# Layer 2 of a two-layer mixture of experts written out by hand, and partial token tiles collected

## The chip, the cores and the metric

The kernel runs on one core of one Trainium2 chip. The metric is the device time of one execution in microseconds (us). Before the change the median of three runs is 539.6 us (539.29 to 540.68). The engines are TensorE (PE; its weight loads are listed as PEld), VectorE (DVE), ScalarE (ACT), GpSimd (POOL) and SyncE (SP), which here only issues DMAs.

## The reference, cut to what matters

An attention without softmax (the scores are multiplied by a decay) gives 2304 tokens of 512 numbers. They pass two layers of a mixture of eight experts: the first has a capacity, the second a skip gate. In both each token goes to the one expert with the highest logit.

```python
logits = x @ w_gate
expert_idx = np.argmax(logits, axis=1)
...
h = np.maximum(np.einsum('ecd,edf->ecf', disp, w1), 0.0)
y = np.einsum('ecf,efd->ecd', h, w2)
...
out[i] = gate_w[i] * y[expert_idx[i], pos[i]]
...
# second layer, on tokens with x @ w_skip > 0; the others keep x
h = np.maximum(xc[mask] @ w1[e], 0.0)
y[mask] = gate_w[mask, None] * (h @ w2[e])
...
out[do_compute] = xc + y
```

Each expert has `w1` of 512 x 1024 and `w2` of 1024 x 512; all numbers are float32.

## The kernel before, in words

Up to some 110 us the kernel computes the attention and the routing of layer 1; layer 1 runs to about 350 us, layer 2 to about 532. Tokens are scattered by an indirect DMA from GpSimd into one list per expert in DRAM (`xs1`, `xs2`), and gathered from there (`load_rows`, L691: `xb`, for the matmuls; `load_own`, L717: `rows`, with gate, token number and, in layer 2, the row itself).

*Positions.* The experts are taken in nine positions (`CAPS`, L31), each with a fixed number of rows: 160, 176, 316, 296, 292, 288, 276, 264, 256 in layer 1 and 176, 32, 324, 240, 172, 172, 156, 156, 144 in layer 2. Positions 0 and 1 are the same expert: 0 takes the rows that are known early, 1 the late ones; position 1 of layer 2 has 32 rows and a path of its own (`SMALL`, `small1`, `small2`). From position 2 on the experts come in order of their number of tokens, which `order` (L542) works out once a layer's routing is complete; `expert` (L681) has SyncE read an expert's number. `ends` writes a block of zero rows behind each list (`pad`, L488, an indirect DMA).

*Steps.* A position has eight steps f, one for each 128 of the 1024 hidden numbers. `s1` (L803) is the first matmul, `h` in PSUM, from which ScalarE makes the ReLU `hh` and, where it is wanted, VectorE the rest `hl`. `s2` (L867) is the second, accumulated in four PSUM tiles `y` (features by tokens), or, for 240 rows, in tiles of tokens (`token_major`). The weights come in units of 512 KB + 512 KB, each for two steps (`load_unit`, L736), five in flight.

*Precision.* Over 192 rows (`F32_MAX`) each float32 factor is split in a high and a low half of type fp32r, and three products are summed: `convert_unit` (L750) makes `hi` (ScalarE, L768) and `lo` (VectorE, L769) of both weights, `transposes` (L783) transposes the rows on VectorE and splits them likewise. Up to 192 rows plain float32 is used. For the positions in `PAIR` (L46: position 1 of layer 1, positions 4 to 7 of layer 2) the second matmul alone is split: both halves of `hh` lie side by side, so that `hi` takes 2C columns at once (L892) and `lo` C more (L893).

*The end of a position.* `evac` (L907) copies `y` to `yt`; `out` (L921) transposes `yt` by tiles of 128 tokens back to rows (`yr`), a tile being four transposes; the last tile of a position is partial. In layer 1 `post1` (L999) computes the scores for the next router (`logits4`, tile `M`; one transpose `Mt` for each token tile), scales the rows by the gate into `x2s` and `x2r` on ScalarE, and scatters both, one indirect DMA for each and each tile. In layer 2 `post2` (L1038) makes the row numbers `of` and `oi` on VectorE (L1050, L1051), then four multiply-adds for each tile (L1056) and one scatter to the output.

*Order.* One loop, `run` (L936), writes out both layers: loads, conversions, gathers, `s1` a step ahead, `s2`. Of this order GpSimd and SyncE keep what is written; TensorE, VectorE and ScalarE are ordered by the planner of the language, by its own costs. Each engine then works off its queue strictly in that order.

## Time and profile before

| | us |
|---|---|
| median of three runs | 539.6 |
| the profiled execution | 540.63 |
| its span, first to last instruction | 538.8 |
| TensorE busy | 514.2 |
| VectorE busy | 328.5 |
| ScalarE busy | 242.2 |
| GpSimd busy | 150.9 |

The mean granted TensorE clock was 0.989 of full speed. A matmul's listed time is longer than the distance to the next one, since they are pipelined: what a step costs is read from the starts of two like instructions, or from the chain of waits, which counts each up to the next.

### The profile page before, as it was taken

What the parts mean: (1) busy time and instruction counts of PE and PEld (TensorE: products, weight loads), DVE (VectorE), ACT (ScalarE), POOL (GpSimd) and SP (SyncE); (2) the same over time, 40 slices, a digit from 0 to 9 for tenths busy, and PEclk for the clock granted to TensorE, in tenths of its full rate; (3) what the DMA queues carried; (4) which work ended last, traced back from release to release, by engine and by line L of the source; (5) the groups of instructions that cost most, each with busy time, mean ns of one, the idle gap of its engine ahead of it and who ended that gap; (6) DMA issues with size and microseconds to landing.
All of it is one profiled execution on the core that took longest, in us unless ns stands there. A gap on an engine that the chain in (4) does not pass through costs nothing.

```text
span 538.8 us, 12402 instructions
## 1 busy us (share of the span) xinstructions
PE 514.2 (95%) x4439; PEld 480.9 (89%) x4439; DVE 328.5 (61%) x992; ACT 242.2 (45%) x448; POOL 150.9 (28%) x216
## 2 busy tenths in 40 slices
PE   7899999999999999999999999998989799999993
PEld 6779888798999999999999999997978689999993
DVE  5756769555775856667585957345667355565422
ACT  2344455243564655656474756234344324344220
POOL 3443747331403060323324242230302110110111
PEclk9999999999999999999999999999989899999998
DMA  8799996855994757584839474317899658788700
GB/s 195 159 204 200 237 233 165 301 192 179 298 285 134 233 167 201 170 230 134 246 112 273 138 245 129 119 46 209 259 350 321 195 197 262 250 276 283 259 25 28
DMA packets 133420, 109.65 MB, mean 203 GB/s; under 512 B 57398, under 2 KB 111030, under 8 KB 133350
## 3 DMA queue, kind: packets, MB, share of 16 engines
q1 hardware_dynamic: 127077, 94.70, 61.5%
q0 software_dynamic: 6272, 14.07, 7.1%
q8 instruction: 37, 0.61, 0.5%
q14 instruction: 34, 0.27, 0.2%
HBM read 93.44 MB, written 20.17 MB: 211 GB/s over the span
## 4 chain that ended last, share of the span: by engine, by line
PE 63%; issue 16%; DMA 8%; SPq 5%; POOL 3%; DVE 2%; ACT 2%; POOLq 0%; DVEq 0%; ACTq 0%
PE h L834 6%; PE h L833 6%; PE h L832 6%; PE y L899 6%; PE y L900 6%; PE y L898 6%; PE h L822 6%; PE yr L929 2%; DMA rows<-xs 2%; PE S L206 2%; PE O L248 2%; PE y L892 2%; PE y L895 2%; DMA r<-w1b 2%; POOL out L986 1%
## 5 line engine op out<-in xcount | busy, mean ns | idle before, releaser
L769 DVE TENSOR_TENSOR lo<-r,hi 128x1024 fp32r<-128x1024 f32 x92 | 112.2, 1223 | 58.3 <-ACT hi L768 57.7
L768 ACT CAST hi<-r 128x1024 fp32r<-128x1024 f32 x92 | 96.3, 1048 | 56.8 <-PE y L899 16.9
L899 PE MATMUL y<-hl,hi 128*128 128x316 f32 (+7 forms) x256 | 76.4, 299 | 0.0
L900 PE MATMUL y<-hh,lo 128*128 128x316 f32 (+7 forms) x256 | 76.2, 298 | 0.0
L898 PE MATMUL y<-hh,hi 128*128 128x316 f32 (+7 forms) x256 | 75.1, 298 | 0.0
L476 POOL DMA_INDIRECT xs<-x2s,idx x24 | 28.0, 1165 | 156.1 <-ACT hi L768 57.7
L837 ACT ACTIVATE hh<-h 128x316 fp32r<-128x316 f32 (+8 forms) x72 | 29.1, 404 | 63.9 <-PE h L834 63.6
L986 POOL DMA_INDIRECT out<-o,oi x17 | 19.7, 1157 | 131.4 <-DVE o L1056 128.4
L892 PE MATMUL y<-hh,hi 128*128 128x312 f32 (+2 forms) x160 | 49.4, 369 | 0.4
L899 PEld LDWEIGHTS y<-hl,hi 128*128 128x128 f32 x256 | 48.2, 188 | 0.3 <-DVE oi L1051 0.2
L900 PEld LDWEIGHTS y<-hh,lo 128*128 128x128 f32 x256 | 48.2, 188 | 0.3 <-issue 0.3
L838 DVE SCALAR_TENSOR_TENSOR hl<-h,hh 128x316 fp32r<-128x316 f32 (+8 forms) x72 | 31.9, 446 | 26.9 <-ACT hh L837 26.8
L898 PEld LDWEIGHTS y<-hh,hi 128*128 128x128 f32 x256 | 47.9, 188 | 0.0
L893 PE MATMUL y<-hh,lo 128*128 128x156 f32 (+2 forms) x160 | 38.5, 240 | 0.0
L209 DVE TENSOR_TENSOR P<-S,tab 128x512 f32<-128x512 f32 (+1 forms) x40 | 23.6, 632 | 15.4 <-PE S L206 15.1
L825 ACT ACTIVATE hh<-h 128x172 fp32r<-128x172 f32 (+2 forms) x40 | 12.4, 310 | 43.3 <-PE h L822 42.5
L892 PEld LDWEIGHTS y<-hh,hi 128*128 128x128 f32 x160 | 30.1, 188 | 1.4 <-DVE hh L826 1.1
L893 PEld LDWEIGHTS y<-hh,lo 128*128 128x128 f32 x160 | 30.5, 191 | 0.1
L895 PE MATMUL y<-hh,r 128*128 128x160 f32 (+2 forms) x192 | 29.9, 300 | 0.0
L986 POOL DMA_INDIRECT out<-x2r,si x24 | 27.7, 1153 | 7.3 <-issue 5.5
L895 PEld LDWEIGHTS y<-hh,r 128*128 128x128 f32 x192 | 27.2, 190 | 0.1
L929 PE MATMUL yr<-ident,yt 128*128 128x128 f32 (+11 forms) x156 | 24.4, 282 | 0.8 <-DVE o L1056 0.8
(613 smaller groups left out, 1268.8 us busy)
## 6 DMA issues: line engine op xcount, KB each, us to landing
r<-w1a SPq DMA_DIRECT2D x32, 512.0 KB
r<-w2a SPq DMA_DIRECT2D x32, 512.0 KB
r<-w1b SPq DMA_DIRECT2D x32, 512.0 KB
r<-w2b SPq DMA_DIRECT2D x32, 512.0 KB
k<-k SPq DMA_DIRECT2D x32, 128.0 KB
q<-q SPq DMA_DIRECT2D x16, 256.0 KB
v<-v SPq DMA_DIRECT2D x32, 128.0 KB
xb<-xs SPq DMA_DIRECT2D x12, 160.0 KB
```

Of the source, the lines that this page charges most:

```text
L768: nc.scalar.copy(hi, raw)
L769: nc.vector.tensor_sub(lo, raw, hi.bitcast(F32))
L822: nc.tensor.matmul(ps, w.r1[:, c, fc], s.xh[:, c, 0:C], start=(c == 0), stop=(c == 3))
L832: nc.tensor.matmul(ps, w.hi1[:, c, fc], s.xh[:, c, 0:C], start=(c == 0), stop=False)
L892: nc.tensor.matmul(s.y[d][:, 0:2 * C], w.hi2[:, f % 2, dc], s.hh[f].rearrange("p a c -> p (a c)"), start=a, stop=False)
L893: nc.tensor.matmul(y, w.lo2[:, f % 2, dc], s.hh[f][:, 0], start=False, stop=o)
L895: nc.tensor.matmul(y, w.r2[:, f % 2, dc], s.hh[f], start=a, stop=o)
L898: nc.tensor.matmul(y, wh, s.hh[f], start=a, stop=False)
L899: nc.tensor.matmul(y, wh, s.hl[f], start=False, stop=False)
L900: nc.tensor.matmul(y, wl, s.hh[f], start=False, stop=o)
L929: g.nc.tensor.transpose(ps[0:n, 128 * d:128 * d + 128], s.yt[:, d, 128 * k:128 * k + n], g.ident)
L986: r = g.nc.gpsimd.indirect_dma_start(out=g.oa["out"][:, :].rearrange("n (b d) -> (n b) d", b=parts), out_offset=IndirectOffsetOnAxis(ap=id ...
```

## The change

Four things are changed.

- Partial token tiles are collected. In groups of positions (`ENDS`: 0 and 1, 2 and 3, 4 to 6 of layer 1; 0 and 2, 4 to 6, 7 and 8 of layer 2) `evac` copies the rows beyond a multiple of 128 into a common tile `cy` (ScalarE); the last position of the group puts it out as one tile, and `load_own` gathers its rows from each expert of the group. In layer 1 the scores of `cy` take a `logits4` call of their own.
- The halves side by side stay in positions 4 and 5 of layer 2 (172 rows). The other three positions of `PAIR` use plain float32.
- Layer 2 has a routine of its own, `run2`, with conversions by halves (`convert_half`: 1 for `w1`, 2 for `w2`). In its context ScalarE and VectorE too keep the order that is written. TensorE is still ordered by the planner, and in layer 1 so are ScalarE and VectorE.
- `of` and the row numbers are computed by GpSimd, and `post(2)` of layer 2 is put out in two parts. `hold` copies the small position's result out of PSUM.

```diff
-TILES = {l: [(c + 127) // 128 for c in cs] for l, cs in CAPS.items()}
+ENDS = {1: [(0, 1), (2, 3), (4, 5, 6)], 2: [(0, 2), (4, 5, 6), (7, 8)]}
+TAIL = {l: {m[-1]: [(p, sum(CAPS[l][q] % 128 for q in m[:i])) for i, p in enumerate(m)] for m in ms} for l, ms in ENDS.items()}
+AT = {l: {p: o for m in ms.values() for p, o in m} for l, ms in TAIL.items()}
...
+def tail(lay, pos):
+
+    return sum(CAPS[lay][p] % 128 for p, _ in TAIL[lay].get(pos, []))
+
+
+TILES = {l: [c // 128 + (p in TAIL[l]) if p in AT[l] else (c + 127) // 128 for p, c in enumerate(cs)] for l, cs in CAPS.items()}
...
-PAIR = {1: (1,), 2: (4, 5, 6, 7)}
+PAIR = (4, 5)
...
+    k = C // 128
+    if T > k:
         nc.gpsimd.memset(s.rows[:, T - 1, GATE - c0:], 0.0)
...
+    if T > k:
+        for p, o in TAIL[lay].get(pos, [(pos, 0)]):
+            m = CAPS[lay][p]
+            n, a = m % 128, start_slot(lay, p) + m - m % 128
+            nc.sync.dma_start(out=s.rows[o:o + n, k], in_=xs[ds(expert(g, lay, p), 1), a:a + n, c0:c1].rearrange("o p w -> (o p) w"))
...
+def convert_half(g, u, i):
...
     if u >= 2 * UNITS:
         return
     lay, pos = user(u)
-    both = CAPS[lay][pos] > F32_MAX
-    if not both and max(pos, 1) not in PAIR[lay]:
+    if CAPS[lay][pos] <= F32_MAX and (i == 1 or lay == 1 or pos not in PAIR):
...
+    raw, shape = (t.r1, [128, 4, 256]) if i == 1 else (t.r2, [128, 2, 512])
+    if hasattr(t, f"hi{i}"):
         return
...
+    hi = g.wc.tile(shape, F32R, tag=f"hi{i}", name=f"hi{i}_{u}")
+    lo = g.wc.tile(shape, F32R, tag=f"lo{i}", name=f"lo{i}_{u}")
+    setattr(t, f"hi{i}", hi)
+    setattr(t, f"lo{i}", lo)
+    nc.scalar.copy(hi, raw)
+    nc.vector.tensor_sub(lo, raw, hi.bitcast(F32))
+
+
+def convert_unit(g, u):
+    convert_half(g, u, 1)
+    convert_half(g, u, 2)
...
-    def transposes(self, pos, cs=range(4)):
+    def transposes(self, pos, cs=range(4), apart=False):
...
-        if not f32:
+        if f32:
+            return
+
+        def high():
             nc.scalar.copy(s.xh[:, c], x)
+
+        def low():
             nc.vector.tensor_sub(s.xl[:, c], x, s.xh[:, c].bitcast(F32))
+
+        if apart:
+            return high, low
+        high()
+        low()
...
+    def pair(self, pos):
+        return self.lay == 2 and pos in PAIR
...
+        if pos in AT[self.lay]:
+            o, n = AT[self.lay][pos], C % 128
+            if o == 0:
+                self.cy = g.yp.tile([128, 4, 128], F32, tag="cy", name=f"cy{self.lay}_{pos}")
+            g.nc.scalar.copy(self.cy[:, :, o:o + n], s.yt[:, :, C - n:C])
+
+    def count(self, pos, k):
+
+        C = CAPS[self.lay][pos]
+        return tail(self.lay, pos) if k == C // 128 and pos in AT[self.lay] else min(128, C - 128 * k)
...
-        n = min(128, C - 128 * k)
+        n = self.count(pos, k)
...
+        y = self.cy[:, :, 0:n] if k == C // 128 and pos in AT[self.lay] else s.yt[:, :, 128 * k:128 * k + n]
         for d in range(4):
-            g.nc.tensor.transpose(ps[0:n, 128 * d:128 * d + 128], s.yt[:, d, 128 * k:128 * k + n], g.ident)
+            g.nc.tensor.transpose(ps[0:n, 128 * d:128 * d + 128], y[:, d], g.ident)
         return n, ps
...
-            base = first_unit(lay, pos)
+            base = first_unit(1, pos)
+            last = pos == NST - 1
+            nx, np_ = (self.next, 0) if last else (self, pos + 1)
...
-                            convert_unit(g, base + 4 if lay == 2 else base)
+                        load_units(g, min(u + LA, base + 4))
                     else:
-                        load_units(g, u + (4 if pos == 1 else LA if (lay, pos) == (1, 2) else LA2))
+                        load_units(g, u + (4 if pos == 1 else LA if pos == 2 else LA2))
                         convert_unit(g, u + 1)
...
+                if f == 2 and pos == 0 or f == 4 and last:
+                    nx.gather(np_)
+                if f == 6 and pos < NST - 2:
+                    self.gather(pos + 2)
+                if last or pos == 0:
+                    if f == 6:
+                        nx.transposes(np_, [0, 1])
+                        nx.transposes(np_, [2, 3])
+                elif f in (2, 4):
+                    nx.transposes(np_, [f - 2, f - 1])
+                if f < 7:
+                    self.s1(pos, f + 1)
+                else:
+                    nx.s1(np_, 0)
                 self.s2(pos, f)
...
+    def run2(self, left, ends):
+
+        g = self.g
+        half = lambda u, i: convert_half(g, u, i)
+        base = lambda pos: first_unit(2, pos)
+        B = base(2)
+        for f in range(8):
+            if f == 0:
+                expert(g, 2, 2)
+                load_units(g, B)
+                self.gather(SMALL)
+                self.gather(2)
+            if f == 2:
+                left()
+            if f == 3:
+                ends()
+            if f == 5:
+                half(B, 1)
+            if f == 6:
+                self.transposes(SMALL, [0, 1])
+                self.transposes(SMALL, [2, 3])
+            if f < 7:
+                self.s1(0, f + 1)
+            if f == 5:
+                half(B, 2)
+            if f == 7:
+                parts = [self.transposes(2, c, apart=True) for c in ([0, 1], [2, 3])]
+                for i in (0, 2, 4, 6):
+                    self.s1(SMALL, i)
+            self.s2(0, f)
+        self.evac(0)
+        for i in (0, 1):
+            for x in parts:
+                x[i]()
+        self.post(0)
+        for f in range(8):
+            if f % 2 == 0:
+                load_units(g, B + f // 2)
+            self.s2(SMALL, f)
+        self.hold(SMALL)
+        self.st[SMALL].rest()
+        self.s1(2, 0)
+        for f in range(8):
+            u = B + f // 2
+            if f == 0:
+                self.gather(3)
+            if f == 6:
+                self.gather(4)
+            if f % 2 == 0:
+                load_units(g, u + LA2)
+                half(u + 1, 1)
+            if f == 1:
+                load_own(g, 2, 2, self.st[2])
+            if f < 7:
+                self.s1(2, f + 1)
+            else:
+                self.s1(3, 0)
+                self.s1(3, 1)
+                half(B + 5, 1)
+            if f % 2 == 0:
+                half(u + 1, 2)
+            if f == 3:
+                self.post(SMALL)
+            if f == 5:
+                parts = [self.transposes(3, c, apart=True) for c in ([0, 1], [2, 3])]
+                for i in (0, 1):
+                    for x in parts:
+                        x[i]()
+            self.s2(2, f)
+        self.evac(2)
+        self.post(2, range(2))
+        for f in range(8):
+            u = B + 4 + f // 2
+            if f % 2 == 0:
+                load_units(g, u + LA2)
+            elif f < 5:
+                half(u + 2, 1)
+            if f == 2:
+                self.gather(5)
+            if f < 6:
+                self.s1(3, f + 2)
+            else:
+                self.s1(4, f - 6)
+            if f % 2 == 0:
+                half(u + 1, 2)
+            if f == 0:
+                self.post(2, range(2, TILES[2][2]))
+            if f == 5:
+                self.transposes(4, [0, 1])
+                self.transposes(4, [2, 3])
+            self.s2(3, f)
+        self.post(3)
+        for pos in range(4, NST):
+            for f in range(8):
+                u = base(pos) + f // 2
+                if f % 2 == 0:
+                    load_units(g, u + LA2)
+                if f == 2 and pos < NST - 2:
+                    self.gather(pos + 2)
+                if f in (2, 4) and pos < NST - 1:
+                    self.transposes(pos + 1, [f - 2, f - 1])
+                if f < 7:
+                    self.s1(pos, f + 1)
+                elif pos < NST - 1:
+                    self.s1(pos + 1, 0)
+                if f % 2 == 0:
+                    half(u + 1, 2)
+                self.s2(pos, f)
+            self.evac(pos)
+            self.post(pos)
+
+    def hold(self, pos):
+
+        g, s = self.g, self.st[pos]
+        y = g.hp.tile([128, 128], F32, tag="ys", name="ysb", bufs=1)
+        g.nc.scalar.copy(y, s.y[0])
+        s.y = [y]
...
+        F, G = 128 * (C // 128) if pos in AT[1] else C, tail(1, pos)
+        if F + G < W:
+            nc.gpsimd.memset(l4[:, F + G:W], 0.0)
...
-        logits4(g, s.yt, g.wg2, [C], l4, f"M4_{pos}_", (3, 2, 1, 0))
+        logits4(g, s.yt, g.wg2, [F], l4, f"M4_{pos}_", (3, 2, 1, 0))
+        if G:
+            logits4(g, l1.cy, g.wg2, [G], l4[:, F:], f"M4_{pos}t", (3, 2, 1, 0))
...
-    def post2(pos):
+    def post2(pos, tiles=None):
         s, T = l2.st[pos], TILES[2][pos]
...
-        f, x = g.rt.tile([128, T], F32, tag="of", name=f"of{pos}", bufs=4), g.rt.tile([128, T], I32, tag="oi", name=f"oi{pos}", bufs=4)
-        v_.tensor_scalar(out=f, in0=s.rows[:, :, VAL], scalar1=-BIG, scalar2=BIG, op0=ALU.mult, op1=ALU.add)
-        v_.tensor_add(x, f, s.rows[:, :, TOK])
-        for k in range(T):
+        if tiles is None or tiles[0] == 0:
+            f, s.to = g.rt.tile([128, T], F32, tag="of", name=f"of{pos}", bufs=4), g.rt.tile([128, T], I32, tag="oi", name=f"oi{pos}", bufs=4)
+            nc.gpsimd.tensor_scalar(out=f, in0=s.rows[:, :, VAL], scalar1=-BIG, scalar2=BIG, op0=ALU.mult, op1=ALU.add)
+            nc.gpsimd.tensor_add(f, f, s.rows[:, :, TOK])
+            nc.gpsimd.tensor_copy(s.to, f)
+        for k in tiles or range(T):
             n, ps = l2.out(pos, k)
             o = g.rt.tile([128, D], F32, tag="xr", name=f"o{pos}_{k}", bufs=6)
...
-            scatter(g, x[0:n, k:k + 1], o[0:n])
+            scatter(g, s.to[0:n, k:k + 1], o[0:n])
...
-    l1.s1(0, 0)
-    l1.run({1: r1.over, NST - 3: r2.pick_first, NST - 2: r2.close_first}, {(0, 0): g.step3, (0, 3): r1.order, (0, 4): r1.ends})
-    l2.run({2: leave2}, {(0, 4): lambda: (load_own(g, 2, 2, l2.st[2]), l2.st[SMALL].rest()), (0, 5): r2.ends})
+    with g.tc.manual_schedule(engines={mybir.EngineType.Pool, mybir.EngineType.SP}):
+        l1.s1(0, 0)
+        l1.run({1: r1.over, NST - 3: r2.pick_first, NST - 2: r2.close_first}, {(0, 0): g.step3, (0, 3): r1.order, (0, 4): r1.ends})
+    with g.tc.manual_schedule(engines={mybir.EngineType.Pool, mybir.EngineType.SP, mybir.EngineType.DVE, mybir.EngineType.Activation}):
+        l2.run2(leave2, r2.ends)
```

## Rows read from the trace of the kernel before

**Rows 1.** Busy time by stretch: stretch, length, then us (instructions) by engine, clock, DMA, GB/s.

```profile
130.00:150.00 20.00, 18.99 (x130) 17.15 (x130) 13.87 (x42) 10.73 (x22) 6.26 (x10) 1.00 0.90 257
160.00:360.00 200.00, 199.88 (x1540) 192.64 (x1539) 131.79 (x388) 111.49 (x190) 58.89 (x83) 1.00 0.59 175
360.00:440.00 80.00, 72.87 (x625) 67.58 (x624) 44.36 (x88) 30.21 (x51) 12.36 (x15) 0.96 0.78 243
440.00:520.00 80.00, 79.83 (x585) 77.01 (x584) 45.12 (x114) 29.64 (x66) 10.43 (x13) 1.00 0.74 244
```

**Rows 2.** Timeline of TensorE, 370 to 430 us: start, length, instruction, [idle before, releaser].

```profile
374.50 0.41 PE L832 MATMUL h<-x_2h,hi 128*128 128x324 f32 x1 [0.90 <-ACT hi L768]
...
375.76 0.42 PE L834 MATMUL h<-x_2h,lo 128*128 128x324 f32 x1 [0.70 <-DVE lo L769]
...
392.93 0.41 PE L832 MATMUL h<-x_2h,hi 128*128 128x324 f32 x1 [1.67 <-ACT hi L768]
...
394.19 0.63 PE L834 MATMUL h<-x_2h,lo 128*128 128x324 f32 x1 [0.41 <-DVE lo L769]
...
413.44 0.60 PE L929 MATMUL yr<-ident,yt 128*68 128x128 f32 x4 [0.75 <-DVE o L1056]
...
427.66 0.50 PE L886 MATMUL y<-hi,hl 128*128 128x512 f32 x1 [2.71 <-DVE hl L838]
```

**Rows 3.** Timeline of SyncE's DMA issues, 360 to 386 us.

```profile
360.56 4.52 SPq L702 DMA_DIRECT2D xb<-xs  x8
365.33 0.39 SPq L746 DMA_DIRECT2D r<-w1b  x1
...
382.64 1.97 SPq L702 DMA_DIRECT2D xb<-xs  x4
...
385.93 0.39 SPq L746 DMA_DIRECT2D r<-w1b  x1
```

**Rows 4.** Timeline of ScalarE at 391 us.

```profile
391.83 1.04 ACT L768 CAST hi<-r 128x1024 fp32r<-128x1024 f32 x1 [1.13 <-DMA r<-w1b]
```

**Rows 5.** Timeline of VectorE at 425 us.

```profile
425.75 0.17 DVE L1050 TENSOR_SCALAR of<-rows 128x2 f32<-128x2 f32 x1 [7.49 <-DMA rows<-xs]
```

**Rows 6.** Busy time by stretch, in the two stretches of low granted clock.

```profile
394.20:397.80 3.60, 3.60 (x14) 3.60 (x15) 2.51 (x3) 2.24 (x4) 0.00 (x0) 0.53 1.06 369
...
428.00:431.60 3.60, 3.60 (x17) 3.33 (x16) 2.59 (x4) 1.04 (x1) 0.00 (x0) 0.55 0.43 108
```

**Rows 7.** Chain of waits, 349 to 354 us: start, time up to the next, what.

```profile
349.62 0.57 PE M L329 x8
...
350.99 0.22 PE Mt L342 x2
351.20 0.99 PE yr L929 x8
352.19 1.20 PE y L895 x8
```

**Rows 8.** Timeline of TensorE: like instructions of two steps, at 176 and 156 rows.

```profile
136.69 0.45 PE L892 MATMUL y<-hh,hi 128*128 128x352 f32 x1
...
138.98 0.44 PE L892 MATMUL y<-hh,hi 128*128 128x352 f32 x1
...
500.17 0.24 PE L893 MATMUL y<-hh,lo 128*128 128x156 f32 x1
...
502.25 0.24 PE L893 MATMUL y<-hh,lo 128*128 128x156 f32 x1
```

**Rows 9.** Timeline of GpSimd, 200 to 202 us.

```profile
200.55 1.25 POOL L1008 COPY tok<-rows 128x3 f32<-128x3 f32 x1
201.75 0.18 POOL L1017 COPY x2s<-rows 128x6 f32<-128x6 f32 x1
```

**Rows 10.** Timeline of VectorE at the same time.

```profile
200.53 1.23 DVE L769 TENSOR_TENSOR lo<-r,hi 128x1024 fp32r<-128x1024 f32 x1 [1.65 <-ACT hi L768]
```

**Rows 11.** Timeline of VectorE at a change of position, 461 us.

```profile
461.02 1.12 DVE L1056 SCALAR_TENSOR_TENSOR o<-yr,rows 128x128 f32<-128x128 f32 x4
```

More of the change, by code (lines that the diff above doesn't have):

```diff
@@ L1385, in build @@
             g.misc = pc.enter_context(tc.tile_pool(name="psM", bufs=2, space=PSUM))
-            with tc.manual_schedule(engines={mybir.EngineType.Pool, mybir.EngineType.SP}):
-                moe(g)
+            moe(g)
         mc.close()
```

55 lines of the change are left out of this document (5 added, 50 removed).

## The prediction

> **What bounds the kernel now.** I read first the busy time by stretch [rows 1]. TensorE bounds the kernel: in the middle of layer 1 (160 to 360 us) it rests 0.1 us in 200, in the last third of layer 2 (440 to 520) 0.2 us in 80. So there only less TensorE work saves time, and ScalarE, VectorE and GpSimd, at most two thirds busy, cost nothing. The exceptions are 130 to 150 us, with 1.0 us of rest, and 360 to 440 us, with 7.1 us of rest at a mean granted clock of 0.96. Next I read TensorE's order of instructions from 360 to 440 us for what it waited for [rows 2]: six waits, 0.90 + 0.70 + 1.67 + 0.41 + 0.75 + 2.71 = 7.14 us, the whole rest of the stretch. Last I followed the longest back.
>
> The 1.67 and 0.41 us are the first-step weights of layer 2's position 2, third unit: ScalarE's `hi` stood until its load landed at 391.8 [rows 4]. SyncE issued that load only at 385.93 [rows 3], since the gather for position 3, which waited for the pad rows, stood before it in its queue until 382.64. The 0.90 and 0.70 us are the first unit of that position, whose load left at 365.33, behind two gathers. The 2.71 us is VectorE: a tiny `of`, put early into its order by the planner, waited 7.49 us for a gather [rows 5], and the `hl` that TensorE needed stood behind it. The 0.75 us is the third output tile of position 2, for which no PSUM buffer was free. After the 1.67 + 0.41 us and after the 2.71 us the granted clock was 0.53 and 0.55 for 3.6 us each [rows 6], about the lower of its two levels, 1.2 of 2.4 GHz.
>
> **The change part by part**, against the profiled execution: 540.63 us, span 538.8.
>
> *Waits of layer 2.* In `run2` the first unit's load goes out at step 0 of position 0, ahead of both gathers, whose first issue was at 360.56 [rows 3] for want of rows; it is behind only the reading of the expert's number. Its conversions come at step 5. During the small position loads follow with no gather between them, and `ends` comes before `load_own` and `rest` instead of behind, so that the pad rows no longer wait for those. The third unit then stands behind no gather (before, behind the one that left at 382.64) and no row loads, only behind the buffers that the small position gives free. `of` and its index go to GpSimd; `post(2)` makes two tiles, then the third a step later. So each of the six waits loses what caused it: -7.1 us.
>
> *Half clock.* With the waits gone so is what preceded the low clock: 3.6 x (1 - 0.53) + 3.6 x (1 - 0.55) = 1.7 + 1.6, -3.3 us.
>
> *Tiles.* Collecting tails makes the token tiles of layer 1 20 instead of 24, and drops 4 of layer 2's 18. Two tiles take 0.99 us of TensorE for `yr` and, in layer 1, 0.22 us for `Mt` [rows 7], so 0.50 and 0.11 us each: 4 x 0.61 + 4 x 0.50 = -4.4 us. It is in the stretches where TensorE never rests, so all of it counts. The ScalarE, VectorE and GpSimd work of those tiles (two copies and two scatters, or four multiply-adds and one scatter) lies beside it and is counted at nothing, as are the 14 added copies into `cy`: the three engines are at most 69% busy in every stretch [rows 1].
>
> *Router scores.* Tails add three `logits4` calls; the columns stay the same (160 + 176 = 128 + 128 + 80). A call on 256 columns takes 0.57 us [rows 7]. If all is per column the price is 0, if all is per call 3 x 0.57 = 1.7. Four column tiles share the array, so I hold it near the first: +0.5 us.
>
> *Halves side by side.* Position 1 of layer 1 (176 rows) and positions 6 and 7 of layer 2 (156) go back to plain float32. One step with halves takes 138.98 - 136.69 = 2.29 us at 176 rows and 502.25 - 500.17 = 2.08 at 156 [rows 8]. Plain: four output tiles at 176 rows take 1.20 us [rows 7], the first matmul of the step has as many passes, so 2.40, and 2.40 x 156/176 = 2.13. Price (0.11 x 8) + (0.05 x 16) = +1.7 us. Dropped are 4 + 8 conversions of 1.04 us on ScalarE [rows 4] and their VectorE half. In layer 2 they lay under a full TensorE: nothing. In layer 1 they stand in the stretch with 1.0 us of rest; I give back 0.6 of it (0 to 1.0).
>
> *New waits.* VectorE and ScalarE now take layer 2 in program order, so behind an instruction that waits stands all that follows. Two places are tight. At the end of position 0 VectorE has in order `lo` of the first unit, the small transposes, the transposes of position 2 (which wait for the second gather, issued in the second half of the eight issues from 360.56 [rows 3]), the small `ht` and the emptying of PSUM. If the gather is late, all of these and TensorE's small second step wait. The earlier weight load also shares the DMA engines with the scatters on which the gathers wait. The other is each change of position: the multiply-adds of the finished one, 1.12 us for a tile [rows 11], come before the next one's second `hh`. No row shows this order. The nearest: these changes before cost 0.2 us in 80 [rows 1], and the worst wait was 2.71 us [rows 2] with 1.6 of low clock. So from 0 to 2 x (2.71 + 1.6) = 8.6; I take +1.7, nearer to the first, as at most changes one tile fewer is to be done than before. The tail is left as it is: the last tiles are still two.
>
> On moving `of` to GpSimd: a GpSimd copy of three columns took 1.25 us where one of six took 0.18 [rows 9], and in those 1.25 us VectorE ran a subtraction of two SBUF tensors, 1.23 us [rows 10]. GpSimd waits for that in slack. What VectorE loses when GpSimd is first is at most 24 small reads x 0.18 = 4.3 us, spread over 180 us. The Trainium skill (SBUF — State Buffer, "Who interferes with whom") says that a VectorE instruction with two SBUF inputs and a GpSimd one that reads SBUF exclude each other, and the later one waits for the whole of the other; it speaks against this move, and the trace agrees on the one side. By it the sum would be up to 4.3 us worse if every meeting stood on the path; by the rows, where VectorE is 56% busy, I add nothing.
>
> Sum: -7.1 - 3.3 - 4.4 + 0.5 + 1.7 - 0.6 + 1.7 = -11.5, so 529.1 for an execution like the profiled one. The median lies 1.0 us under that one (539.6 to 540.63): 528.1 us.
>
> **The rivals.**
> (1) *The waits come back elsewhere.* The gather of position 2 heads VectorE's queue too early, and planner and hand order disagree in one or two places, each with a low clock behind it: one wait of 2.7 + 1.6 and a few of half a microsecond, 6 in all instead of 1.7. For it: the six waits had different causes, and the program order is fixed where arrival is not. Against: the loads start earlier, and the DMA engines are at 0.78 in 360 to 440 us [rows 1]. It gives 528.1 + 4.3 = 532.4, up to 536.
> (2) *The order doesn't do it.* TensorE is still placed by the planner, so its waits and low clock stay and only the work terms are left: -4.4 + 0.5 + 1.7 - 0.6 = -2.8, so 536.8. Against: the causes are named in other queues than TensorE's, and each is moved.
> (3) *Slower: convoys at the changes of position.* ScalarE's ReLU of the next position stands behind the copy into `cy`, which stands behind VectorE's additions; VectorE's `hh` stands behind multiply-adds that wait for TensorE's `yr`. If TensorE has run out of matmuls by then, each of seven changes costs a wait as long as the 1.67 us after which the clock fell, and 1.6 of low clock: 7 x 3.3 = 23, so 528.1 - 1.7 + 23 = 549. It is slower from five such changes on (5 x 3.3 = 16.5 is over the 13.2 gained). Against: with two tiles at each change TensorE rested 0.2 us in 80.
>
> **How the numbers follow.** Forecast 0.66, rival 1 0.20, rival 2 0.05, rival 3 0.07; 0.02 for anything else. Without any new wait and with the lower ends (router scores 0, all 1.0 us of the early rest) it is 525.5; with a third more saved on the tiles, 524. Above, rival 1 reaches 536. The range is 524 to 536. A measurement tells 0.3% apart, 1.6 us: under 538.0 is faster, over 541.2 slower. Faster takes the forecast, rival 1 and most of rival 2, 0.89; slower rival 3 and some of the rest, 0.08; within 0.3% 0.03.
>
> **What would show it.** In the profile after: TensorE rests under 2 us between 350 and 440, and the granted clock is near 1.00 there until the last tiles; the third unit's load well ahead of 382.64; no VectorE instruction that waits for a row load ahead of an `hl`; 32 fewer `yr` and 4 fewer `Mt` transposes; steps of 156 rows of 2.1 us. The prediction is wrong if TensorE shows new waits over 1 us at the start of position 2 or at changes of position, or if layer 1, whose ScalarE and VectorE are still placed by the planner, got waits it did not have.

## The result, and the profile after

The changed kernel takes 531.43 us (median, 529.96 to 533.73) where the kernel before took 539.44 beside it (538.50 to 540.68): a ratio of 0.985, 95% interval 0.982 to 0.988. Faster, as forecast, and inside the range, but 3.3 us above the forecast of 528.1. The profiled execution is the fastest one, 529.96 us with a span of 528.1 and a mean granted clock of 0.994; the sum had given 529.1 for an execution like the profiled one of before. The two profiled executions lie 10.7 us apart, the medians 8.0, since the profile before is of an execution 1.0 us above its median and the one after of an execution 1.5 us under its own. What the stages below show is thus 2.7 us more than the median gained.

First the busy time by stretch, against [rows 1] (columns as there).

```profile
130.00:150.00 20.00, 19.34 (x133) 18.34 (x132) 10.04 (x35) 7.74 (x18) 3.64 (x8) 1.00 0.95 251
160.00:360.00 200.00, 199.26 (x1543) 192.71 (x1542) 130.06 (x364) 110.03 (x191) 52.68 (x72) 1.00 0.60 175
360.00:440.00 80.00, 77.51 (x677) 72.49 (x676) 48.42 (x90) 32.35 (x58) 16.17 (x26) 1.00 0.88 263
440.00:520.00 80.00, 79.60 (x596) 78.02 (x594) 22.79 (x60) 20.39 (x59) 8.34 (x18) 1.00 0.70 220
```

In 360 to 440 us TensorE's rest fell from 7.1 to 2.5 us and the clock rose from 0.96 to 1.00. In the timeline of TensorE all six waits of [rows 2] are gone. Three short ones, 0.26 to 0.52 us, stand in layer 1, and in layer 2 one new, at the start of position 2:

```profile
130.67 0.41 PE L339 MATMUL M<-yt,wg 128*32 128x128 f32 x2 [0.52 <-DVE yt L946]
...
373.04 0.89 PE L969 MATMUL yr<-ident,yt 128*128 128x128 f32 x4 [2.20 <-ACT yt L948]
```

It is the place that the prediction called tight. The timeline of VectorE shows why:

```profile
370.52 1.71 DVE L811 STREAM_TRANSPOSE x_2f<-xb 128x704 f32<-128x704 f32 x2 [3.79 <-DMA xb<-xs]
372.15 0.33 DVE L885 STREAM_TRANSPOSE ht<-hr 128x64 f32<-128x64 f32 x2
```

The transposes of position 2 stand 3.79 us for the gather, and behind them, in program order, the small `ht` and the emptying of PSUM that TensorE wanted. The chain of waits says why the gather was late:

```profile
355.99 0.51 issue
356.53 0.42 issue
356.95 5.54 DMA xs<-x2s,idx
362.51 0.35 SPq L712
...
366.16 4.17 DMA xb<-xs
370.52 1.71 DVE x_2f L811 x2
```

The last scatter of layer 1 took 5.54 us to land, and no gather can leave before it. At 356.29, 0.7 us ahead of that scatter, SyncE had issued the load that the change moved forward:

```profile
356.29 0.40 SPq L759 DMA_DIRECT2D r<-w1b  x1
356.92 0.38 SPq L760 DMA_DIRECT2D r<-w2b  x1
362.51 3.98 SPq L712 DMA_DIRECT2D xb<-xs  x8
```

So the first gather left at 362.51 instead of 360.56 [rows 3]. The third unit's load now leaves at 368.07 and 374.56 instead of 385.93 [rows 3].

Where the time went, from the first `h` matmul of each position, after less before: start of layer 1 -0.3 us; its stages, position 1 to position 8: -1.0, +0.4, -0.7, +0.6, -0.5, -0.5, +1.0, +0.1; start of layer 2 -0.9; start of position 2 of layer 2 +1.2; of position 3 -5.2; of position 4 -9.1; of position 6 -9.9; TensorE's end -11.0.

### The profile page after: what moved, and what is told of

It is laid out like the page before. It is cut to its first block, busy times and chain, and to the rows that moved or that the text cites. A ratio compares the mean times of both kernels' runs of the same rounds, so it can differ in the third digit from the quotient of the medians.

```text
span 528.1 us, 12239 instructions
## 1 busy us (share of the span) xinstructions
PE 508.8 (96%) x4427; PEld 478.4 (91%) x4427; DVE 299.4 (57%) x914; ACT 226.7 (43%) x440; POOL 144.4 (27%) x216
## 4 chain that ended last, share of the span: by engine, by line
PE 79%; DMA 6%; DVE 5%; SPq 4%; issue 3%; POOL 2%; ACT 1%; POOLq 0%; DVEq 0%; ACTq 0%
PE h L848 11%; PE y L924 7%; PE h L860 7%; PE h L859 7%; PE h L858 7%; PE y L928 6%; PE y L929 6%; PE y L927 6%; PE yr L969 3%; SPq L151 2%; DMA v<-v 2%; PE y L921 2%; PE S L216 2%; PE O L258 2%; PE xps L656 1%
## 5 line engine op out<-in xcount | busy, mean ns | idle before, releaser
L780 DVE TENSOR_TENSOR lo<-r,hi 128x1024 fp32r<-128x1024 f32 x80 | 97.7, 1223 | 55.9 <-ACT hi L779 53.4
L779 ACT CAST hi<-r 128x1024 fp32r<-128x1024 f32 x80 | 83.6, 1048 | 34.2 <-PE y L928 20.0
L924 PE MATMUL y<-hh,r 128*128 128x176 f32 (+3 forms) x384 | 60.5, 301 | 0.0
L924 PEld LDWEIGHTS y<-hh,r 128*128 128x128 f32 x384 | 55.0, 190 | 0.1
L929 PEld LDWEIGHTS y<-hh,lo 128*128 128x128 f32 x256 | 48.3, 189 | 0.0
L927 PEld LDWEIGHTS y<-hh,hi 128*128 128x128 f32 x256 | 47.7, 188 | 0.2
L855 ACT ACTIVATE hh<-h 128x176 f32<-128x176 f32 (+3 forms) x48 | 14.7, 305 | 73.8 <-PE h L848 73.1
L183 POOL TENSOR_TENSOR vh<-v,tab 128x512 f32<-128x512 f32 x15 | 15.7, 1046 | 29.0 <-PE O L258 15.0
L848 PE MATMUL h<-x_0h,r 128*128 128x160 f32 (+1 forms) x128 | 22.7, 311 | 0.0
L236 DVE TENSOR_TENSOR st<-st,kv 64x64 f32<-64x64 f32 x96 | 20.9, 218 | 3.0
```

The costliest lines, as they stand in the source:

```text
L779: nc.scalar.copy(hi, raw)
L780: nc.vector.tensor_sub(lo, raw, hi.bitcast(F32))
L848: nc.tensor.matmul(ps, w.r1[:, c, fc], s.xh[:, c, 0:C], start=(c == 0), stop=(c == 3))
L924: nc.tensor.matmul(y, w.r2[:, f % 2, dc], s.hh[f], start=a, stop=o)
L927: nc.tensor.matmul(y, wh, s.hh[f], start=a, stop=False)
L929: nc.tensor.matmul(y, wl, s.hh[f], start=False, stop=o)
```

## The experiments

Two theories to begin with. **A:** layer 2's gain comes from ScalarE and VectorE being in program order, as the change's name says; what is missing to the forecast is the new wait and the low clock behind it. **B:** the gain comes from the loads and gathers, which were moved, and from `of`; the order by hand is at best neutral. The first four kernels ran on one chip (kernel before 540.4 us, 537.1 to 543.5), the other eight on another, where the kernel before took 553.2 us; those are compared among themselves, and the ratios that their expectations name, taken from the first chip, don't hold there. The diffs are cut to what matters. "Of the means" gives the difference of two means with its 95% interval; a position's stage runs from its first `h` matmul to that of the next position.

**1. The change once more** (no edit).

> The changed kernel once more, to see what lies behind its spread (530.0 to 533.7 us in six runs, where the profiled one took 530.0). Theory A: the 2.20 us wait of TensorE at the start of layer 2's position 2 is always there, and in the longer runs the granted clock falls after it, which before cost 1.6 to 1.7 us for each stretch; then a profile of a longer run shows a stretch of some 3.6 us near 0.55 behind 373 us and nothing else, and the runs keep to 530 to 534. Rival: the spread is spread over the whole kernel (DMA arrivals, the last scatters); then the profile shows all position starts shifted by small amounts and no low clock.

532.27 us (531.05 to 533.58), ratio 0.985 (0.981 to 0.989). The trace is the same up to the wait (2.26 us), then differs. By stretch, TensorE first:

```profile
372.00:376.00 4.00, 2.94 (x58) 2.61 (x62) 2.62 (x9) 2.47 (x7) 1.91 (x5) 0.83 1.01 318
376.00:380.00 4.00, 4.00 (x35) 3.62 (x27) 1.53 (x6) 0.83 (x3) 1.20 (x3) 0.75 0.96 344
```

In the profile of the section above both stretches have 1.00. Position 3 starts 1.6 us later than there, and so does all that follows. The wait is therefore 2.2 us long, and 3.8 us are lost where the clock drops behind it.

**2. The load of unit 36 behind the gathers**, its conversions behind the emptying.

```diff
-                expert(g, 2, 2)
-                load_units(g, B)
                 self.gather(SMALL)
                 self.gather(2)
+                load_units(g, B)
...
-            if f == 5:
-                half(B, 1)
...
         for i in (0, 1):
             for x in parts:
                 x[i]()
+        half(B, 1)
+        half(B, 2)
```

> Undoes one move: the load of position 2's first unit stands behind the two gathers again, and its two conversions stand behind the emptying of position 0, since before that its weights can't be there. Theory A (the load shares the DMA engines with the two scatters that the gathers wait for): the last scatter lands in about 2.7 us instead of 5.54, the gathers leave about 2 us earlier than 362.5, the transposes of position 2 no longer wait (3.79 us before), and the 2.20 us wait of TensorE goes; in its place stands a wait for the unit's hi and lo of 1.5 to 3 us, so that the time stays within 1.5 us of the changed kernel's. Rival: the scatters are slow for another reason (their own descriptors); then they still land in about 5 us, the 2.20 us wait stays, the hi wait is added, and the time is 2 to 4 us longer.

529.95 us (529.43 to 532.38, 4 runs), ratio 0.981 (0.976 to 0.986). In the chain of waits the scatter lands in half the time:

```profile
358.06 2.73 DMA xs<-x2s,idx
360.80 0.34 SPq L712
```

and TensorE has, for the wait of 2.20, two short ones, for the conversions that are now late:

```profile
375.20 0.42 PE L858 MATMUL h<-x_2h,hi 128*128 128x324 f32 x1 [0.53 <-ACT hi L779]
...
376.46 0.42 PE L860 MATMUL h<-x_2h,lo 128*128 128x324 f32 x1 [0.40 <-DVE lo L780]
```

So the early load does lengthen the scatter, and through it the gather. The two short waits are 0.93 us together, where 1.5 to 3 were expected, though the load leaves as late as in the kernel before: at 365.58 us, 19.1 us after the start of layer 2 in both. From the start of layer 2 to that of position 3 it takes 56.3 us, the change 57.3 and 59.0 without and with low clock; of the means it is 1.9 us under run 1, give or take 2.0. So once its conversions stand behind the emptying, moving this load forward has no gain that these runs can tell.

**3. The transposes of position 2 behind the emptying of position 0.**

```diff
-                parts = [self.transposes(2, c, apart=True) for c in ([0, 1], [2, 3])]
                 for i in (0, 2, 4, 6):
                     self.s1(SMALL, i)
             self.s2(0, f)
         self.evac(0)
+        parts = [self.transposes(2, c, apart=True) for c in ([0, 1], [2, 3])]
```

> Moves one thing: the two VectorE transposes of position 2 stand behind the small position's transposes and the emptying of position 0. Theory A (the 2.20 us wait is a convoy: instructions whose input was there stood on VectorE behind the two transposes that waited for the gather): TensorE goes on with yr and the small second step (2.8 us together) while the gather lands, the wait shrinks to under 1 us, position 2 starts 1 to 2 us earlier, and the time falls by 1 to 2.5 us (more where a low clock followed). Rival: position 2 is bound by the gather itself; the wait only moves behind the small step, in front of position 2's first matmul, position 2 starts within 0.5 us of where it did, and the time stays the same.

530.28 us (529.30 to 532.20), ratio 0.982 (0.978 to 0.985). The early load and the slow scatter are kept, yet the wait is gone; what is left is a pause inside the small second step, for which the profile shows no releaser:

```profile
375.16 0.95 PE L893 MATMUL ys<-r,ht 128*32 128x128 f32 x25 [0.81 <-issue]
```

To position 3 it takes 56.1 us, 1.3 less than the change without low clock and 2.9 less than with it; of the means it is 1.7 us under run 1, give or take 1.3. So what cost time was not the late gather but what stood behind it in VectorE's queue.

**4. Halves side by side as before** in position 1 of layer 1 and 6 and 7 of layer 2; `cy` is 116 columns wide, to make room (as in runs 5 and 10).

```diff
-PAIR = (4, 5)
+PAIR = {1: (1,), 2: (4, 5, 6, 7)}
```

> Undoes one part: the halves stand side by side again in position 1 of layer 1 and positions 6 and 7 of layer 2 (a spare width of one buffer is cut to make room, which changes no work). By the prediction's terms TensorE gains 0.9 us at 176 rows and 0.8 at 156, and the early stretch loses 0.6 us to its conversions: 1.1 us faster than the changed kernel, steps of 156 rows of 2.08 us. Rival: the conversions that come back in program order on ScalarE and VectorE cost more than the matmuls gain; the same or up to 2 us slower, with TensorE waits named hi, lo or hh between 465 and 505 us or between 128 and 150 us.

530.84 us (529.60 to 533.05), ratio 0.983 (0.979 to 0.986). The stages of positions 6 and 7 fall from 17.76 and 17.96 to 17.44 and 17.80 us: plain float32 costs 0.5 us there, where the sum had 0.8; the stage of position 8 gives 0.18 of it back (18.99 against 18.81). Position 1 of layer 1 takes 22.24 us, with two waits of TensorE as the rival said (0.85 us for `oh`, 0.66 for `hh`). With plain float32 it took 21.70 in the result, and 21.69, 22.64 and 22.41 in runs 1 to 3, so neither is shown to be shorter there. Of the means the run is 1.2 us under run 1, give or take 1.4: not told apart. The wait before position 2 was 2.85 us, with no low clock behind it:

```profile
374.35 0.89 PE L969 MATMUL yr<-ident,yt 128*128 128x128 f32 x4 [2.85 <-ACT yt L948]
...
374.00:378.00 4.00, 3.65 (x74) 3.12 (x75) 2.84 (x8) 2.49 (x7) 1.50 (x4) 1.00 0.88 284
```

**5. Layer 1 with its tail tiles one by one.**

```diff
-ENDS = {1: [(0, 1), (2, 3), (4, 5, 6)], 2: [(0, 2), (4, 5, 6), (7, 8)]}
+ENDS = {1: [], 2: [(0, 2), (4, 5, 6), (7, 8)]}
```

> Layer 1 alone loses its collected tails (its tail tiles are worked one by one again, so 4 more groups of M and none of the added logits4 calls and cy copies); layer 2 stays as changed. Theory (layer 1 gained only 0.6 to 0.9 us of the 1.9 that the terms gave, because the three added M groups and the planner's placing behind them took 1 to 1.3 us back): the time rises by 0.4 to 1.2 us against the changed kernel, ratio to the kernel before 0.986 to 0.988, and the stages of positions 2, 4 and 7 of layer 1 get shorter by 0.4 to 1 us while those of positions 1, 3, 5 and 6 get longer. Rival (the terms were right and something else delayed layer 1, such as the wait at 130 us, whose length hangs on the arrival of a weight load): 1.9 us slower, ratio 0.989, and positions 2, 4 and 7 do not get shorter by more than the router scores' 0.17 us each.

543.61 us (540.10 to 544.96), some 3.7 us above run 8 on the same chip, more than either side allowed. Part of it is another thing: ScalarE's conversion came late to position 6,

```profile
294.33 1.05 ACT L779 CAST hi<-r 128x1024 fp32r<-128x1024 f32 x1 [1.89 <-remote]
```

and at 324 to 326 us TensorE waited twice more (0.60 and 0.93 us), with a clock of 0.57 behind it in 326 to 330. Of the stages free of that, 3 and 5 take 29.63 and 28.63 us where run 9 took 28.74 and 27.82, so a tile dropped is worth 0.8 to 0.9; 2 and 4 take 29.81 and 28.65 where run 9 took 30.14 and run 11 29.11, so the stage behind an added `logits4` call loses 0.3 to 0.5 (position 4 of run 9 had a wait of 0.68 us of its own). Both figures include the router columns that the change moves from a position to the last of its group. And with its tiles one by one, layer 1 still takes 0.1 to 0.3 us more than the kernel before in each of the stages of positions 2 to 5, 0.8 in all, though the changed kernel's stages of positions 2, 3 and 5 are the same on both chips to 0.02 us: that part is not the tails. The total is not decided by this run.

**6. Layer 2 with its tail tiles one by one.**

```diff
-ENDS = {1: [(0, 1), (2, 3), (4, 5, 6)], 2: [(0, 2), (4, 5, 6), (7, 8)]}
+ENDS = {1: [(0, 1), (2, 3), (4, 5, 6)], 2: []}
```

> Layer 2 alone loses its collected tails (3 groups of yr more per group, so 4 more groups of 4 transposes and 4 more stt); layer 1 and the program order stay as changed. Theory (a yr group of 0.22 to 0.99 us that runs on TensorE between other matmuls lengthens the path in full): 2.0 us slower than the changed kernel, ratio 0.988 to 0.990, found in the layer 2 stages after positions 0, 4, 5 and 7. Rival (at position changes TensorE would have waited anyway, so what it does there is free): within 0.4 us of the changed kernel.

540.48 us (539.26 to 541.92): 0.6 above run 8 and level with run 9, where 2.0 were expected. The stages behind positions 4 and 5 are each 0.48 us longer (19.17 and 18.24 against 18.69 and 17.76), as the 0.50 for a tile said. That behind position 7 is 0.14 longer, and behind position 0 two tiles take 1.18 us in TensorE's timeline where one took 0.89:

```profile
380.42 1.18 PE L969 MATMUL yr<-ident,yt 128*128 128x128 f32 x8 [2.54 <-ACT yt L948]
```

That makes 0.48 + 0.48 + 0.14 + 0.29 = 1.4 of the 2.0 us. In the time it doesn't show: this profile had no low clock behind the wait, those of runs 8 and 9 had, and position 4 of layer 1, which the edit leaves alone, took 29.09 us here and 30.08 and 30.05 there. Theory in part, then; the rival holds for the tile of position 7.

**7. ScalarE and VectorE of layer 2 left to the planner**, the moved loads and gathers kept.

```diff
-    with g.tc.manual_schedule(engines={mybir.EngineType.Pool, mybir.EngineType.SP, mybir.EngineType.DVE, mybir.EngineType.Activation}):
+    with g.tc.manual_schedule(engines={mybir.EngineType.Pool, mybir.EngineType.SP}):
```

> Layer 2 written out as in the change, loads and gathers at the same places, but ScalarE and VectorE are ordered by the planner again. Theory (what removed the 7.1 us of TensorE waits and the 3.3 us of half clock of layer 2 is the order on ScalarE and VectorE): TensorE waits of together 3 to 8 us come back between position 2 and position 4 of layer 2, the clock falls there, the time is 533 to 541 us, ratio 0.990 to 1.000. Rival (it was the place of the loads and gathers, and of the index work on GpSimd, that removed them): within 1 us of the changed kernel, ratio 0.983 to 0.987, no wait above 1 us past the one before position 2.

537.96 us (536.50 to 539.61). Run 9, the changed kernel on the same chip in the next set, took 540.55: without the order by hand it is not slower but 2.6 us faster (of the means 3.0, give or take 1.6). Theory A falls. The planner puts the same transposes behind the first of VectorE's emptying, as run 3 did by hand, and TensorE waits less for them:

```profile
380.43 0.57 PE L858 MATMUL h<-x_2h,hi 128*128 128x324 f32 x2 [1.31 <-ACT x_2h L816]
...
418.12 0.62 PE L969 MATMUL yr<-ident,cy 128*116 128x128 f32 x4 [0.67 <-DVE o L1204]
```

From the start of layer 2 to that of position 3 it takes 56.4 us, run 9 59.5. From there on the order by hand is 0.6 us shorter (116.9 against 117.5): the second line is the third tile of position 2, for which TensorE waited 0.75 us in [rows 2] and, by hand, not at all. So the order by hand cures that one wait, and loses more at the start of position 2.

**8. `of` back on VectorE**, in program order.

```diff
-            nc.gpsimd.tensor_scalar(out=f, in0=s.rows[:, :, VAL], scalar1=-BIG, scalar2=BIG, op0=ALU.mult, op1=ALU.add)
-            nc.gpsimd.tensor_add(f, f, s.rows[:, :, TOK])
-            nc.gpsimd.tensor_copy(s.to, f)
+            v_.tensor_scalar(out=f, in0=s.rows[:, :, VAL], scalar1=-BIG, scalar2=BIG, op0=ALU.mult, op1=ALU.add)
+            v_.tensor_add(s.to, f, s.rows[:, :, TOK])
```

> The tokens' target rows (of and its conversion, three small operations per position) go back from GpSimd to VectorE, at the place that the program order gives them; all else as in the changed kernel. Theory (in the kernel before these waited at the head of VectorE's queue for rows only because the planner had put them early; in program order the rows have long landed): within 0.5 us of the changed kernel, ratio 0.983 to 0.987, and no VectorE instruction waits for rows by more than 0.5 us in layer 2. Rival (VectorE still waits for rows ahead of an hl): 1 to 4 us slower, with a wait on the rows' load shown on VectorE and one on hl shown on TensorE.

539.88 us (535.99 to 542.16), level with the changed kernel. The row that stood 7.49 us in [rows 5] is now

```profile
441.44 0.16 DVE L1197 TENSOR_SCALAR of<-rows 128x2 f32<-128x2 f32 x1
```

without a wait. So with the order by hand the move to GpSimd buys nothing that these runs can tell (of the means run 9 is 1.3 us longer, give or take 2.2).

**9. The change a third time**, on this chip, beside the next three.

> The changed kernel itself, beside the next three on the same chip. Ratio to the kernel before 0.983 to 0.988; in its profile a wait of TensorE of 2.0 to 2.9 us ahead of the yr before position 2 of layer 2, and no other wait above 0.7 us from there to the end.

540.55 us (539.21 to 542.97), ratio 0.979 (0.974 to 0.984), under the 0.983 to 0.988 expected. The wait is 2.74 us, the clock 0.61 in 382 to 386.

**10. Late transposes, and halves in positions 6 and 7.** The edit of run 3, and

```diff
-PAIR = (4, 5)
+PAIR = (4, 5, 6, 7)
```

> The changed kernel with two alterations: the transposes of position 2's rows stand behind the emptying of position 0 on VectorE, and positions 6 and 7 of layer 2 keep their halves side by side (as in the kernel before). Theory (the wait before position 2 costs 1.4 us and at times a stretch of low clock more, and the halves save 0.5 us in positions 6 and 7): 1.9 to 3.5 us faster than the changed kernel. Rival for the transposes (the wait only moves to the row halves that position 2 needs): as fast as the changed kernel within 0.5 us. Rival for the halves (their conversions delay hh or hl): the stages of positions 6 and 7 are no shorter than 17.7 and 18.0 us.

537.32 us (533.60 to 539.98), ratio 0.973 (0.967 to 0.978); of the means it is 3.9 us under run 9, give or take 2.6, where 1.9 to 3.5 were expected. The wait before `yr` is gone; the pause in the small second step is 1.27 us here, and the clock is 1.00 from 376 to 388. Positions 6 and 7 take 17.42 and 17.80 us against 17.76 and 17.96. This version is faster than the kernel before and the changed one.

**11. Loads and gathers as before, order by hand kept.**

```diff
             if f == 0:
-                expert(g, 2, 2)
-                load_units(g, B)
                 self.gather(SMALL)
-                self.gather(2)
             if f == 2:
+                self.gather(2)
                 left()
-            if f == 3:
+            if f == 4:
+                load_units(g, B)
+                load_own(g, 2, 2, self.st[2])
+                self.st[SMALL].rest()
+            if f == 5:
                 ends()
...
                 load_units(g, B + f // 2)
+            if f == 2:
+                self.gather(3)
```

> ScalarE and VectorE of layer 2 in program order and of on GpSimd, as in the changed kernel; but SyncE's and GpSimd's order at the start of layer 2 is put back as before: unit 36's load behind both gathers, the row loads of the small position and of position 2 ahead of the pad rows, and the gather for position 3 ahead of the third unit. Theory (the place of loads and gathers decides, not the order on ScalarE and VectorE, as the run with the planner's order pointed to): TensorE waits for hi and lo of position 2's first and third unit come back, 2 to 4 us together, with a low clock behind the longer one; 2 to 6 us slower than the changed kernel. Rival (the transposes were the rest of it, and with the program order the loads have enough slack): within 1 us of the changed kernel.

The two conversions of the first unit also stand a step later, at step 6 of position 0. 545.09 us (542.23 to 547.06), 4.5 above run 9 (of the means 4.1, give or take 2.0); in the profiles layer 2 is 3.3 us longer. The price is as expected, the place is not: the third unit is never waited for. The first one is, by ScalarE, and in program order a ReLU stands behind it:

```profile
376.48 1.04 ACT L779 CAST hi<-r 128x1024 fp32r<-128x1024 f32 x1 [5.41 <-DMA r<-w1b]
377.43 0.31 ACT L855 ACTIVATE hh<-h 128x176 f32<-128x176 f32 x1
```

In TensorE's timeline that is

```profile
377.80 0.86 PE L924 MATMUL y<-hh,r 128*128 128x176 f32 x4 [3.56 <-ACT hh L855]
```

and by stretch the next 4 us are

```profile
380.00:384.00 4.00, 3.99 (x95) 3.45 (x84) 3.09 (x9) 1.33 (x6) 0.00 (x0) 0.64 0.29 71
```

The load leaves behind both gathers, at 371.47 us, `hi` stands 5.41 us for it, TensorE 3.56 us for the ReLU, and the clock is 0.64 after that. The load left 19.3 us after the start of layer 2, and in run 2 19.1: as late, but there the conversions stood behind the emptying and the price was 0.93 us. So it isn't the late load alone that costs, but the late load with its conversion written ahead of a ReLU that TensorE wants.

**12. The planner's order, and `of` on VectorE.** The edits of runs 7 and 8 together.

> ScalarE and VectorE of layer 2 ordered by the planner, and of back on VectorE; loads and gathers as in the changed kernel. Theory (the wait of 2.71 us for hl came from an of that the planner put early; either the hand order or GpSimd takes it away, and with neither it returns): a VectorE of waits for its rows by over 1 us ahead of an hl or hh, TensorE waits 1 to 3 us for it, and the time is 1 to 4 us above that of the planner's order with of on GpSimd, which stood at 0.9717 of the kernel before on a chip where that took 553 us. Rival (the earlier row loads took that wait away): no such wait, and as fast as the changed kernel or up to 2 us faster.

545.66 us (543.24 to 550.67): 7.7 above run 7, which differs from it by the place of `of` alone, twice what was expected. VectorE's timeline:

```profile
435.49 0.15 DVE L1197 TENSOR_SCALAR of<-rows 128x1 f32<-128x1 f32 x1 [10.69 <-DMA rows<-xs]
435.68 0.16 DVE L1198 TENSOR_TENSOR oi<-of,rows 128x1 int32<-128x1 f32 x1
435.76 0.71 DVE L864 SCALAR_TENSOR_TENSOR hl<-h,hh 128x240 fp32r<-128x240 f32 x2
```

TensorE's:

```profile
436.21 0.80 PE L915 MATMUL y<-hi,hl 128*128 128x512 f32 x1 [6.47 <-DVE hl L864]
```

and the stretch behind it:

```profile
436.00:440.00 4.00, 3.79 (x14) 3.32 (x14) 1.92 (x4) 0.00 (x0) 0.00 (x0) 0.50 0.51 154
```

An instruction of 0.15 us, put early by the planner, stands 10.69 us for its rows; TensorE loses 6.47, and the clock is 0.50 behind it. [rows 5] show the same with 7.49 and 2.71.

So on the second chip, from best to worst: 537.3 (late transposes and halves), 538.0 (planner, `of` on GpSimd), 539.9 and 540.6 (by hand, `of` on VectorE or GpSimd), 545.1 (by hand, old loads), 545.7 (planner, `of` on VectorE). The first two are not told apart, nor the last two. A planner's order is as good as one by hand once the one instruction that can stand long is out of VectorE's queue; an order by hand is hurt by a load that leaves late where it has the load's conversion ahead of other work (run 11), and hardly where it has not (run 2).

## Why the prediction was right, and where it was off

**Right: the waits and the half clock of layer 2.** The six waits went, and the low clock of [rows 6] with them: position 2 of layer 2 still starts 1.2 us later than before, position 4 then 9.1 us earlier. In the two profiles layer 2 is 10.1 us shorter up to TensorE's end; the terms for it were -7.1 - 3.3 - 2.0 + 0.8 + 1.7 = -9.9. The cause read in VectorE's queue [rows 5] is shown by run 12, which puts it back and pays 7.7 us. The one read in SyncE's [rows 3] is shown for the first unit by run 11, which pays 4.5 us, with the limit that run 2 sets: the load may leave as late if its conversions are moved. For the third unit [rows 4] it is left open: run 11 put its load back behind a gather, and it was in time. What the prediction didn't separate is which part of the change cures which: for `of` program order or GpSimd, either alone (runs 7 and 8); for the first unit the early load (run 7) or later conversions (run 2); for the third tile of position 2 the program order (run 7).

**Right in kind, too small: the new waits.** The place was named, with the queue (transposes waiting for the second gather, `ht` and the emptying behind them) and with the second cause, the earlier load beside the scatters. The value taken was 1.7 us, between 0 and 8.6. It is 2.2 in the profile of the result and, with the low clock behind it, 3.8 in run 1. Of seven profiles with this wait (2.20 to 2.86 us) four show the low clock, so some executions pay 1.6 us that the profiled one escaped. That this one lies 1.5 us under its median fits, but the others of its set were not traced. The value went by [rows 1], which average over changes of position with no gather in the queue; the row that stood nearer was the gather's late issue at 360.56 [rows 3], on which this queue hangs. With it came what the prediction had itself named as a sign of being wrong: a new wait over 1 us at the start of position 2, and a rest in 360 to 440 us of 2.5 us where under 2 was asked for. So the cures were read rightly, and the step that program order adds few waits was not.

**Off, and partly luck: from the execution to the median.** For an execution like the profiled one the sum gave 529.1, and 529.96 was measured. The last step took 1.0 us off for the median, from where one execution of the kernel before happened to lie; here the median lies 1.5 us above the profiled one. These 2.5 us are most of the 3.3 us by which the forecast fell short, and the close fit of the profiled execution is in part that it was the fastest of six. That the median is inside the range owes to the room left for the first rival.

**Right: the tiles**, by count (`yr` from 156 transposes to 124, `Mt` from 24 to 20) and by the 0.50 us of one in layer 2 (0.48 in run 6), though not each is on the path: those behind positions 0 and 7 brought little, so that run 6 shows 1.4 of the 2.0 us.

**Off: layer 1.** The sum had -2.4 for tiles, +0.5 for router scores, +0.9 for plain float32 and -0.6 for rest, -1.7 together; the stages give -0.6. Position 1 is better than its terms in this profile (-1.0 against -0.3), but not in runs 2 and 3 (0.0 and -0.3), so that gain isn't firm. The three stages behind an added `logits4` call grow by 0.4, 0.6 and 1.0 us, 2.0 in all where the term was 0.5. The timeline of TensorE has the call itself:

```profile
295.69 0.64 PE L339 MATMUL M<-yt,wg 128*32 128x256 f32 x8
296.14 0.34 PE L339 MATMUL M_6t<-cy,wg 128*32 128x88 f32 x8
```

From start to start the 256 columns take 0.45 us and the 88 0.27, so a part is per call. But over all of layer 1 these matmuls take 5.6 us from start to start where they took 5.5 before: the calls themselves cost 0.1 us of TensorE, less than the term. What else makes these stages grow is in part the columns moved into them (32, 60 and 68, which the stages before lose); the rest, over 1 us, no run separates. The stage of position 7 lost most: there the planner put the six scalings of the finished position (298.25 to 301.8 us) ahead of the next ReLU on ScalarE, and TensorE stuttered; that they do so because of the added call is argued, not shown. And the other condition for being wrong was met in small: layer 1 got a wait at 130.67, as the planner now puts a conversion that stands 1.26 us for a weight load, and its `lo`, ahead of the emptying. It was 0.52 us there, 0.5 to 1.5 in the other runs without halves in layer 1 (before, TensorE waited 0.68 us for `x2s` in this position).

**Off, small: halves in positions 6 and 7**, 0.5 us (runs 4 and 10) where 0.8 were set, or 0.3 with what position 8 gives back.

**Of the rivals**, the first came half true: one wait came back at the place named, with its low clock in four of seven profiles. The measured 531.43 lies between the forecast and its 532.4, and nearer to the rival (1.0 us against 3.3). The convoys at other changes of position didn't come: from 376 us to the last tiles TensorE's timeline names no wait in the changed kernel. GpSimd beside VectorE cost nothing that runs 8 and 9 could tell apart (539.88 and 540.55). So of the rule in the Trainium skill (SBUF — State Buffer, "Who interferes with whom") on the two engines' ports, by which up to 4.3 us were set beside the sum, no run here shows a price.

## What to carry to other kernels

In a queue worked off in order, look for the instruction that can stand longest and for what stands behind it: here a 0.15 us instruction cost 7.7 us (run 12) and a pair of transposes 1.3 to 2.9 (runs 1 and 3), where a tile saved is worth 0.1 to 0.9. Put what waits for a transfer behind what the bounding engine wants next, whoever writes the order; and before writing an order by hand, move the loads alone and see what is left. A load moved forward competes with the transfers on which other loads depend, so price those too, and try first whether its conversion can be moved back instead (run 2). A forecast made from one profiled execution is a forecast of one execution: the gain here was 10.7 us by the profiles and 8.0 by the medians.

## What the runs showed of the hardware

A last scatter of layer 1 (`x2s`, an indirect DMA) landed in 2.73 us with no weight load beside it and in 5.54 us with two times 512 KB issued just ahead of it. The profile of the result lists the DMA packets by queue: q1 has SyncE's loads, q0 GpSimd's scatters (packets, MB, share of 16 engines). The first line is all that moved from 359 to 361 us, the others are from 361 to 362.5:

```profile
q1 hardware_dynamic: 468, 0.69, 105.5%
...
q0 software_dynamic: 240, 0.29, 52.5%
q1 hardware_dynamic: 50, 0.07, 12.5%
```

So the scatters were not slowed side by side with the load: for 2 us none of their packets moved, and 240 followed when the load was nearly through. From 358 to 359 us both queues had moved some (250 of q1, 35 of q0). The Trainium skill (DMA: Bandwidth & Descriptors, "Queues, rings and completion order") says that each DMA engine takes its queues in turn, a packet at a time. In those 2 us the trace shows no such turn; whether the packets that it lists are those of the page no run here shows.

A rest of TensorE of 2.2 to 2.9 us was followed by a low granted clock in four profiles (0.58 to 0.63 in the lowest 4 us, so most of it at the lower of its two levels) and by 1.00 in three, and the length of the rest doesn't sort them: 2.85 us (run 4) had none, 2.26 us (run 1) had it.

And the kernel before took 540 us on one chip and 553 on the other, where the change's ratio was 0.979 (0.974 to 0.984) instead of 0.985 (0.982 to 0.988). The kernel before wasn't traced there, the changed one was: of the 10.7 us between its two profiles (the result's and run 9's) 5.9 lie ahead of layer 1, 2.3 in layer 1 and 2.1 ahead of position 2 of layer 2. Why the first are lost isn't shown.
